# Loading a weight matrix in eight pieces instead of three, and sharing the last PSUM copy between VectorE and ScalarE

## The chip, the cores and the metric

The kernel runs on one core of a Trainium2 chip. The metric is device time in microseconds (us) of one execution. All runs named here are fast runs (granted TensorE clock 0.999 to 1.0). The kernel before was timed again beside every group of experiments; its medians lay between 1238.22 and 1238.44 us, single runs between 1238.15 and 1238.86 (the profiled execution took 1238.14). The groups did not all run on one chip, so each kernel is compared with the runs of the kernel before beside it.

## The reference, cut to what matters

Two models run on their own inputs and are joined in the last axis. `A` is a state space layer. `B` is attention over segments with a memory, followed by a projection with `Wo` (32 heads of 128, to 1024 columns). Only this projection is touched by the change:

```python
o = jnp.einsum('bhqk,bhke->bhqe', p, v)
o = jnp.einsum('bhte,hed->btd', o, Wo)      # Wo: (32, 128, 1024), 8 MB in bf16
```

## The kernel before

`Wo` is held as two halves of its columns, 128 partitions x 32 heads x 512 columns each. The first half is loaded early in the attention stage, the second when the buffers of the projections come free:

```python
for n, (hp, u) in enumerate(at):              # attention, one step at a time
    if n == 12:
        k.SP.dma_start(wo0[:], b.Wo[:, :, 0:512])
    # ... cut ...
            if first is None:
                # ... cut: wo1 allocated ...
                b.load_o_early(3)             # a DMA transpose
                for h in range(0, H, 16):
                    k.SP.dma_start(wo1[:, h:h + 16, :], b.Wo[:, h:h + 16, 512:D])
                first = b.outproj_first()     # first users of wo0 and wo1
```

The very last block of 128 rows is computed in three chunks of columns. Each is accumulated over 32 heads in one PSUM tile, copied to SBUF and stored:

```python
def out_last(self, ol):
    ot = self.p4a.tile([128, D], BF16, name="b_ost", bufs=4)
    for i, (c0, c1) in enumerate(((0, 512), (512, 768), (768, 1024))):
        p = k.ps("P")
        for h in range(H):
            k.PE.matmul(p[:, 0:c1 - c0], ol[h][:, 384:512], self.wo[...], start=(h == 0), stop=(h == H - 1))
        k.copy("vsv"[i], ot[:, c0:c1], p[:, 0:c1 - c0])   # v: VectorE, s: ScalarE
        k.SP.dma_start(self.out[0, T - 128:T, D + c0:D + c1], ot[:, c0:c1])
```

After this every engine reads a flag and branches over a fallback path that these inputs don't need.

Of the kernel before, what the change touches and what calls it, by code (L numbers as in the profile page):

```python
# [25 lines left out]
H = 32; E = 128; SEG = 32; M = 8; NSEG = 64; L = M + SEG  # L26
# [326 lines left out]
class PartB:  # L353
# [461 lines left out]
    def out_last(self, ol):  # L815

        k = self.k
        ot = self.p4a.tile([128, D], BF16, name="b_ost", bufs=4)
        for i, (c0, c1) in enumerate(((0, 512), (512, 768), (768, 1024))):
            p = k.ps("P")  # L820
            for h in range(H):
                k.PE.matmul(p[:, 0:c1 - c0], ol[h][:, 384:512], self.wo[c0 // 512][:, h, c0 % 512:c0 % 512 + c1 - c0], start=(h == 0), stop=(h == H - 1))
            k.copy("vsv"[i], ot[:, c0:c1], p[:, 0:c1 - c0])
            k.SP.dma_start(self.out[0, T - 128:T, D + c0:D + c1], ot[:, c0:c1])
            yield

# [188 lines left out]
def kernel_main(tc, A_x, A_Lre, A_Lim, A_Bre, A_Bim, A_Cre, A_Cim, A_logdt, A_Dskip, B_x, B_mem0, B_Wq, B_Wk, B_Wv, B_Wo, out,  # L1015
                force=False, dbg=None):
    with ExitStack() as ctx:
        k = K(tc, ctx)
# [3 lines left out]
        b = PartB(k, B_x, B_mem0, B_Wq, B_Wk, B_Wv, B_Wo, out)  # L1022

        def pool(name, side, bufs=2):
            return tc.tile_pool(name=name, bufs=bufs, side=side, reuse_waits="tile")
# [113 lines left out]
        wo0 = t32.tile([128, H, 512], BF16, name="t32")  # L1139
# [6 lines left out]
        first, b.ol0 = None, []  # L1146
        for n, (hp, u) in enumerate(at):
            if n == 12:
                k.SP.dma_start(wo0[:], b.Wo[:, :, 0:512])
            if hp % 2 == 0 and 2 < hp + 2 < HP:  # L1150
                if u == 4:
                    vm = b.v_mem(hp // 2 + 1)
                if u in (4, 6, 8):
                    next(vm)
            if hp == 13 and u in (3, 6, 9):
                b.load_o_early(u // 3 - 1)
            want = min(18 * HP, LEAD + (n + 1) * 18 // 11)
            while done < want:
                next(pr)
                done += 1  # L1160
            if done == 18 * HP:
                if first is None:
                    xs.close()
                    b.p4a = ctx.enter_context(pool("p4a", "left", 1))
                    wo1 = b.p4a.tile([128, H, 512], BF16, name="wo1")
                    b.wo = (wo0, wo1)
                    b.load_o_early(3)
                    for h in range(0, H, 16):
                        k.SP.dma_start(wo1[:, h:h + 16, :], b.Wo[:, h:h + 16, 512:D])
                    first = b.outproj_first()  # L1170
                next(first)
                next(first)
# [30 lines left out]
@with_exitstack  # L1203
def kernel(
    ctx: ExitStack,
    tc: tile.TileContext,
    A_x: bass.AP,
    A_Lambda_re: bass.AP,
    A_Lambda_im: bass.AP,
    A_B_re: bass.AP,  # L1210
    A_B_im: bass.AP,
    A_C_re: bass.AP,
    A_C_im: bass.AP,
    A_log_dt: bass.AP,
    A_Dskip: bass.AP,
    B_x: bass.AP,
    B_mem0: bass.AP,
    B_Wq: bass.AP,
    B_Wk: bass.AP,
    B_Wv: bass.AP,  # L1220
    B_Wo: bass.AP,
    B_seg_len: bass.AP,
    out: bass.AP,
):
    assert int(B_seg_len) == SEG
    kernel_main(tc, A_x, A_Lambda_re, A_Lambda_im, A_B_re, A_B_im, A_C_re, A_C_im, A_log_dt, A_Dskip,
                B_x, B_mem0, B_Wq, B_Wk, B_Wv, B_Wo, out)
# [35 lines left out]
```

## Time and profile before

| | before |
|---|---|
| time, median of 3 | 1238.22 us |
| span of the profile | 1236.4 us |
| TensorE busy | 1226.7 us, 99% |
| TensorE's waits, all | 1.8 us, none for `Wo` |
| last matmul ends | 1232.23 us |
| last copy (VectorE, 256 columns) | 1232.26 to 1232.68 us |
| from its end to the end of the span | 3.8 us |

With an engine at 99%, the question for any change is what it does to the little time around that engine: here the end, where nothing runs beside the copy, the store and the shutdown. The shutdown is visible when one looks at the line of the final branch. The prediction took the times of the branches from there, but made nothing of SyncE's eight waits; this view of the kernel before (engine and operation, count, durations in ns, first to last start in us) belongs to the experiments below:

```profile
L1197 SPq EVENT_SEMAPHORE  x8: 17/17/17, 1233.6 to 1234.7; - x8
...
L1197 ACTq COMPARE_BRANCH  x1: 58/58/58, 1229.4 to 1229.4; - x1
...
L1197 DVEq COMPARE_BRANCH  x1: 72/72/72, 1232.9 to 1232.9; - x1
```

The first line is SyncE waiting, one after the other, for the eight completion semaphores that go round among its DMAs (in the records of the kernel before, SyncE's 406 issues use eight semaphores, 357 of the 405 steps from one issue to the next go on to the next of the eight, and 362 issues follow a recorded wait for their own semaphore). The others are the final branches: ScalarE's long before the end, VectorE's just after its last copy.

### The profile page before, as it was taken

How to read it: one execution, taken by the hardware profiler on the slowest of the kernel's cores; microseconds unless marked ns; L12 is line 12 of the kernel's file. 1: busy time of each engine (PE TensorE's matmuls, PEld its weight loads, DVE VectorE, ACT ScalarE, POOL GpSimd, SP SyncE). 2: the span in 40 equal slices, each digit the busy share in tenths (PEclk: the TensorE clock that was granted, in tenths of full speed). 3: DMA queues.
4: the chain of work that ended last, by engine and by line, in shares of the span. 5: the costliest groups of instructions: out<-in, count | busy, mean ns of one | idle time of the engine just before them, and what ended most of it. 6: DMA issues, size and time to landing. Idle time of an engine off the chain costs nothing.

```text
span 1236.4 us, 19973 instructions
## 1 busy us (share of the span) xinstructions
PE 1226.7 (99%) x8104; PEld 655.0 (53%) x8174; DVE 680.7 (55%) x1270; ACT 266.6 (22%) x694; POOL 271.8 (22%) x437
## 2 busy tenths in 40 slices
PE   9999999999999999999999999999999999999998
PEld 4444444444455555556666656555665554445444
DVE  4799999998711124666666666666666641001000
ACT  4444444443310000211112211111221110000000
POOL 4111232112322321322222222323222320000000
PEclk9999999999999999999999999999999999999999
DMA  9943455562798834855464645546574279507000
GB/s 246 246 148 93 126 141 143 154 172 89 232 306 258 248 120 95 234 125 139 96 154 109 154 108 135 127 91 132 115 151 97 62 208 234 113 17 154 18 17 27
DMA packets 321268, 174.20 MB, mean 141 GB/s; under 512 B 145882, under 2 KB 308876, under 8 KB 321172
## 3 DMA queue, kind: packets, MB, share of 16 engines
q1 hardware_dynamic: 299076, 145.33, 48.4%
q10 hardware_dynamic: 21072, 24.38, 6.1%
q0 software_dynamic: 1024, 3.17, 0.7%
q8 instruction: 65, 1.06, 0.4%
q14 instruction: 31, 0.25, 0.1%
HBM read 84.42 MB, written 53.96 MB: 112 GB/s over the span
## 4 chain that ended last, share of the span: by engine, by line
PE 94%; DVE 4%; issue 1%; DMA 0%; ACT 0%; SPq 0%; DVEq 0%
PE psP L69 80%; PE psU L69 7%; PE psS L69 3%; PE psO L69 2%; PE psR L69 1%; DVE a_pr L284 1%; DVE a_pr L274 1%; DVE a_pr L279 1%; DMA b_xr<-in_B_x_dram 0%; DVE a_n L299 0%; DVE a_h L302 0%; DVE a_fr L232 0%; DVE a_tabh L243 0%; DVE a_tabh L240 0%; ACT a_g L285 0%
## 5 line engine op out<-in xcount | busy, mean ns | idle before, releaser
L69 PE MATMUL psP<-b_xe,b_wk 128*128 128x480 bf16 (+1 forms) x1280 | 247.5, 343 | 0.0
L69 PE MATMUL psP<-b_xe,b_wq 128*128 128x480 bf16 (+1 forms) x1280 | 247.5, 343 | 0.0
L69 PE MATMUL psP<-b_wv,b_xe 128*128 128x512 bf16 (+2 forms) x1027 | 223.0, 372 | 1.3 <-ACT b_xe L94 0.2
L689 POOL TENSOR_TENSOR b_m<-b_e,maskB 99x396 bf16<-99x396 bf16 (+1 forms) x160 | 134.7, 842 | 335.4 <-ACT b_e L688 335.4
L688 ACT ACTIVATE b_e<-psS 99x396 bf16<-99x396 f32 (+3 forms) x208 | 91.5, 442 | 530.4 <-PE psS L69 530.4
L69 PEld LDWEIGHTS <-b_wk 128*128 128x128 bf16 x1280 | 119.2, 98 | 94.2
L69 PEld LDWEIGHTS <-b_wq 128*128 128x128 bf16 x1280 | 118.5, 98 | 87.7
L69 PEld LDWEIGHTS <-b_xe 128*128 128x128 bf16 x1056 | 101.9, 98 | 119.1 <-ACT b_xe L94 0.4
L96 DVE CAST b_k<-psP 128x480 bf16<-128x480 f32 (+1 forms) x192 | 97.3, 528 | 100.0 <-PE psP L69 100.0
L96 DVE CAST b_q<-psP 128x480 bf16<-128x480 f32 (+1 forms) x192 | 97.3, 529 | 92.2 <-PE psP L69 90.9
L69 PEld LDWEIGHTS <-b_ol 128*128 128x128 bf16 x864 | 84.3, 98 | 94.4
L69 PE MATMUL psU<-a_xT,a_bt 128*128 128x512 bf16 x500 | 114.1, 379 | 0.6
L69 PE MATMUL psP<-t,a_hl 128*128 128x512 bf16 x497 | 112.3, 379 | 0.8
L96 DVE CAST b_ost<-psP 128x512 bf16<-128x512 f32 (+1 forms) x17 | 11.5, 676 | 177.6 <-PE psP L69 176.6
L69 PE MATMUL psP<-wo,b_ol 128*128 128x512 bf16 (+1 forms) x440 | 91.9, 364 | 0.4
L69 PE MATMUL psP<-t,b_ol 128*128 128x512 bf16 x408 | 91.7, 379 | 0.4
L94 ACT ACTIVATE b_vst<-psP 128x512 bf16<-128x512 f32 x126 | 72.5, 589 | 76.0 <-PE psP L69 69.9
L289 POOL TENSOR_SCALAR a_tt<-a_pr,a_tabf 128x1 f32<-128x1 f32 x48 | 34.7, 723 | 245.4 <-DVE a_pr L284 245.4
L706 DVE TENSOR_TENSOR b_ob<-psO,b_accR 99x384 bf16<-99x384 f32 x160 | 86.0, 554 | 2.9 <-DVE b_accR L705 0.4
L69 PEld LDWEIGHTS <-a_bt 128*128 128x128 bf16 x512 | 49.8, 98 | 59.5
L69 PEld LDWEIGHTS <-a_hl 128*128 128x128 bf16 x512 | 49.1, 98 | 56.7
L274 DVE TENSOR_TENSOR a_pr<-psU,a_tabf 128x2048 f32<-128x2048 f32 x32 | 73.1, 2283 | 9.2 <-PE psU L69 9.1
(203 smaller groups left out, 968.5 us busy)
## 6 DMA issues: line engine op xcount, KB each, us to landing
b_v<-b_vx SPq DMA_DIRECT2D x16, 1122.0 KB
b_wv<-in_B_Wv_dram SPq DMA_DIRECT2D x16, 1024.0 KB
b_vx<-b_vst ACTq DMA_DIRECT2D x24, 544.0 KB
b_on<-b_ob SPq DMA_DIRECT2D x15, 720.0 KB
a_hs<-a_h SPq DMA_DIRECT2D x32, 256.0 KB
b_wog<-in_B_Wo_dram SPq DMA_DIRECT2D x4, 2048.0 KB
b_wq<-in_B_Wq_dram SPq DMA_DIRECT2D x16, 512.0 KB
b_wk<-in_B_Wk_dram SPq DMA_DIRECT2D x16, 512.0 KB
```

The source lines that it names most:

```text
L69: r = f(*a, **kw)
L94: self.S.activation(out, in_, ACT.Copy)
L96: self.V.tensor_copy(out, in_)
L274: V.tensor_tensor(pr[:], u[:].unsqueeze(1).to_broadcast([128, 2, 2, TB]), view(t3, [[TB + 1, 2], [TB + 1, 2], [1, TB]]), ALU.mult)
L279: V.tensor_tensor(w, w, pr[:, :, 1, :], ALU.add)
L284: V.tensor_tensor_scan(w[:, j, :], rb, w[:, j, :], 0.0 if ini is None else ini[:, j:j + 1], ALU.mult, ALU.add)
L289: G.tensor_scalar(tt[:, j:j + 1], w[:, j, TB - 1:TB], t3[:, 1, TB:TB + 1], None, ALU.mult)
L688: k.S.activation(e[:, a:b, :, 0:n], s[0:GW, a:b, :, 0:n], ACT.Exp, scale=float(E) ** -0.5, accum_out=self.accE[0:GW, j:j + 1])
L689: k.G.tensor_tensor(mv[:, a:b, :, 0:n], e[:, a:b, :, 0:n], mask[0:GW, :, 0:n].unsqueeze(2).to_broadcast([GW, b - a, 2, n]), ALU.mult)
L706: V.tensor_tensor(self.ob[:, b0:b0 + n, :], o[0:GW, 0:n, 0:E], r.unsqueeze(2).to_broadcast([GW, n, E]), ALU.mult)
```

## The change

The intent: smaller pieces of `Wo` were to be used sooner, and two engines were to copy the last 256 columns in half the time.

```diff
-            k.copy("vsv"[i], ot[:, c0:c1], p[:, 0:c1 - c0])
+            if i < 2:
+                k.copy("vs"[i], ot[:, c0:c1], p[:, 0:c1 - c0])
+            else:
+                k.copy("s", ot[:, c0 + 128:c1], p[:, 128:c1 - c0])
+                k.copy("v", ot[:, c0:c0 + 128], p[:, 0:128])
@@
-                k.SP.dma_start(wo0[:], b.Wo[:, :, 0:512])
+                for h in range(0, H, 8):
+                    k.SP.dma_start(wo0[:, h:h + 8, :], b.Wo[:, h:h + 8, 0:512])
@@
-                    for h in range(0, H, 16):
-                        k.SP.dma_start(wo1[:, h:h + 16, :], b.Wo[:, h:h + 16, 512:D])
+                    for h in range(0, H, 8):
+                        k.SP.dma_start(wo1[:, h:h + 8, :], b.Wo[:, h:h + 8, 512:D])
```

## The prediction

> **What bounds the kernel now.** I read the page first, for the shares of the engines:
>
> ```profile
> PE 1226.7 (99%) x8104; PEld 655.0 (53%) x8174; DVE 680.7 (55%) x1270; ACT 266.6 (22%) x694; POOL 271.8 (22%) x437
> ```
>
> TensorE (PE) is busy for 1226.7 us of a span of 1236.4 us. So at most 9.7 us are idle time of this engine, whatever the loads do. Next I asked who TensorE waits for, over the whole run (columns: engine and what it was about to do, whom it waited for, us in total, times, longest us):
>
> ```profile
> PE psR L69 <- DVE hpb L110: 1.3, 1, 1.3
> PE psU L69 <- DMA b_xr<-in_B_x_dram: 0.3, 1, 0.3
> PE psP L69 <- ACT b_xe L94: 0.2, 1, 0.2
> ```
>
> These are all of its waits, 1.8 us, and none names Wo. The same question asked for 460 to 1237 us, which holds both Wo loads and all their readers, has an empty answer. The rest of the 9.7 us is the launch before the first matmul, small gaps of 0.05 us between matmuls, and the stretch after the last matmul. That end I read from the chain that ended last (start us, us, what):
>
> ```profile
> 1220.97 11.27 PE psP L69 x83
> 1232.23 0.02 issue
> 1232.26 0.42 DVE b_ost L96
> ```
>
> The last matmul ends at 1232.23, one VectorE copy of 0.42 us follows, and the remaining 3.7 us to 1236.4 are the store of 64 KB, its confirmation and the shutdown. So there are two places where this change could act: a wait for Wo, which does not exist, and a copy of 0.42 us.
>
> To see how far Wo is from being waited for, I compared the timeline of the issues on SyncE with that of TensorE. The issues (first half of the columns of Wo, then the second half in two pieces, with a DMA transpose between them):
>
> ```profile
> 510.35 0.37 SPq L69 DMA_DIRECT2D t<-in_B_Wo_dram  x1
> ...
> 999.77 0.40 SPq L69 DMA_DIRECT2D wo<-in_B_Wo_dram  x1
> 1000.27 10.73 SPq L69 DMA_TRANSPOSE b_ol<-b_on  x1
> 1011.06 0.57 SPq L69 DMA_DIRECT2D wo<-in_B_Wo_dram  x1
> ```
>
> The first readers on TensorE (`t` holds the first half, `wo` the second; heads 0 to 15 are multiplied with `b_wv`, 16 to 23 with `b_vst`, 24 to 31 with `b_ol`):
>
> ```profile
> 999.57 1.89 PE L69 MATMUL psP<-t,b_wv 128*128 128x512 bf16 x7
> ...
> 1030.05 3.62 PE L69 MATMUL psP<-wo,b_wv 128*128 128x512 bf16 x16
> 1033.50 1.89 PE L69 MATMUL psP<-wo,b_vst 128*128 128x512 bf16 x7
> ```
>
> The first half is issued 489 us before its first reader. The last piece of the second half is issued 1033.50 - 1011.06 = 22.4 us before its own.
>
> [...]
>
> **The change part by part.**
>
> *Wo, first half.* One DMA of 4096 KB becomes four of 1024 KB, same bytes, same row length of 1 KB, same queue. Three more issues at about 0.4 us are 1.2 us of SyncE, which is free from 510.72 us to its next issue at 517.62. Against 489 us of slack: 0 us.
>
> *Wo, second half.* Two DMAs of 2048 KB become four of 1024 KB. The instruction order shows one piece before the transpose and three after it. So only heads 0 to 7 go before the transpose, where 0 to 15 did; but the total of bytes up to the end of Wo is the same. In busy time by stretches of 5 us the DMA moved 246 to 347 GB/s between 1010 and 1020 us; at 284 GB/s (stretch 1005 to 1010), an estimate, 1 MiB takes 3.7 us. If the three pieces were issued at 1011 as the one is now, 3 MiB would land 11.1 us later, at about 1022; heads 8 to 15 are first read at 1030.05 + 8 x 0.216 = 1031.8, and heads 16 to 23 at 1033.5. Slack 8 us or more, so 0 us on the end.
>
> *Semaphores.* Eight completion semaphores go round among the DMAs of SyncE: each DMA waits for the one eight places earlier. More pieces shift this rotation. In the build the second half's successors, the transposes of `b_ol`, each wait for a piece of Wo. The four that fill the next tile are issued from 1020.90 to 1038.77 (17.87 us) in the kernel before, and that tile is first read at 1057.67, 19 us later. A delay of a few us stays hidden. After the first half the next weights are issued at 530.96 and first read at 565.10, 34 us later. Again 0 us.
>
> *The order on the engines.* TensorE and GpSimd keep the same instructions in the same order, VectorE too with one copy narrowed from 256 to 128 columns; ScalarE has one copy of 128 columns more.
>
> *The last copy.* Durations of the same tile's copies in this trace (columns: engine, line, op, tile, durations in ns min/median/max, then times and forms):
>
> ```profile
> L96 DVE CAST b_ost<-psP x17: 425/692/693, 1019.9 to 1232.3; 128x512 bf16<-128x512 f32 x16, 128x256 bf16<-128x256 f32 x1
> L94 ACT ACTIVATE b_ost<-psP x16: 384/597/598, 1037.2 to 1228.8; 128x512 bf16<-128x512 f32 x15, 128x256 bf16<-128x256 f32 x1
> ```
>
> VectorE: 692 ns at 512 columns, 425 at 256, so 1.043 ns a column and 158 ns fixed; at 128 columns 292 ns. ScalarE: 597 and 384, so 0.832 ns a column and 171 ns fixed; at 128 columns 277 ns. [...] Side by side, the pair would take about 0.29 us against 0.425, a gain of 0.13 us. But in the build the ScalarE copy comes first in the program, waits for TensorE, and **the VectorE copy waits for ScalarE**, and no longer for TensorE; the store waits for VectorE. They run one after the other: 0.277 + 0.03 handoff + 0.292 = 0.60 us, where the handoff is that from ScalarE to VectorE at 1136.32 to 1136.35 us in this trace. Against 0.425 us that is **+0.17 us**, all of it on the path, as nothing runs beside it.
>
> Sum: 0 + 0 + 0 + 0.17 us, from 1238.22 to **1238.4 us**.
>
> **The rivals.** *The copies overlap.* The intent of the change; then the end is 0.13 us earlier, 1238.1 us. Against it stand the wait in the build[...]. *Wo was a hidden limit and its pieces release TensorE earlier.* Then TensorE would show a wait for it; it shows none, and the total of its idle time excludes over 0.8% even if every gap went. *The rearranged queue makes a new wait:* the transposes of `b_ol` or the first pieces come late, because they wait for more semaphores. For it speaks that the DMA share is near 1 from 1015 to 1060 us. If it happened it would cost some us at about 1031 or 1057 us: 1240 to 1243 us. The slacks of 8 and 19 us speak against it. *The longer tail meets the shutdown:* ScalarE's final branch, at 1229.4 us now, moves to about 1232.9; VectorE's is at 1232.9 already and SyncE still waits for the store after it, so ScalarE should not become last. At most some tenths.
>
> **Range and chances.** The three runs before lie within 0.11 us, the known effect is +0.17 us, and an overlap would be -0.13 us. I widen to 1237.7 to 1239.4 for run to run and chip to chip differences and a small part of the third rival. Faster by over 2% is out of reach of the 9.7 us; slower by over 2% would need 25 us of new waits: 1% each at most.
>
> **What would show it.** Right: TensorE's waits unchanged and none naming Wo; the tail with ScalarE at about 0.28 us and VectorE after it at 0.29 us; the span 0.1 to 0.3 us longer; the first `wo` matmul still at about 1030 us. Wrong: two copies starting at the same time (then the wait did not hold), an entry of Wo or `b_ol` among TensorE's waits, the first `wo` matmul moved by over 1 us, or the gap after the last copy changed from 3.7 us.

The sum was 0 + 0 + 0 + 0.17 = +0.17 us, and the 0.17 comes from copies in the trace. The 0.216 us for a matmul of 512 columns is the trace's too: the 16 with `wo` and `b_wv` start at 1030.05 us and the next group at 1033.50.

## The result, and the profile after

The changed kernel took 1238.93 us (median of 4, 1238.75 to 1239.23), the kernel before beside it 1238.26 (1238.2 to 1238.33): +0.67 us, the ranges apart. The ratio is 1.0006 with a 95% interval of 0.9988 to 1.0023. Ratios are the mean time of one kernel's fast runs over that of the other's of the same rounds, so not quite the ratio of the medians. A second measurement later gave 1238.75 against 1238.34, +0.41 us, with ranges that overlap (1238.63 to 1239.18, 1238.21 to 1238.86). So the change, meant to save time, costs about half a microsecond.

TensorE after the change: its share in the page, then all of its waits.

```profile
PE 1226.5 (99%) x8104; PEld 654.5 (53%) x8174; DVE 680.6 (55%) x1270; ACT 266.8 (22%) x695; POOL 271.8 (22%) x437
```

```profile
PE psR L69 <- DVE hpb L110: 1.3, 1, 1.3
PE psU L69 <- DMA b_xr<-in_B_x_dram: 0.7, 1, 0.7
```

There is no wait for `Wo`, as there was none before; only the wait of the launch for `b_xr` is 0.4 us longer, and the 0.2 us for ScalarE are gone. The `Wo` issues in SyncE's timeline:

```profile
510.52 5.90 SPq L69 DMA_DIRECT2D t<-in_B_Wo_dram  x4
...
999.98 0.40 SPq L69 DMA_DIRECT2D wo<-in_B_Wo_dram  x1
1000.49 6.72 SPq L69 DMA_TRANSPOSE b_ol<-b_on  x1
1007.26 3.52 SPq L69 DMA_DIRECT2D wo<-in_B_Wo_dram  x3
```

Behind the shorter first piece the issue of the transpose takes 6.72 us where it took 10.73, and the rest of `Wo` is issued at 1007.26 instead of 1011.06. That buys nothing, as in TensorE's timeline its first reader stands where it stood:

```profile
1030.26 3.62 PE L69 MATMUL psP<-wo,b_wv 128*128 128x512 bf16 x16
```

1030.26 against 1030.05 is the offset of 0.21 us that this execution has from its launch on. Now the end of the chain that ended last:

```profile
1221.18 11.27 PE psP L69 x83
1232.45 0.02 issue
1232.47 0.29 ACT b_ost L94
1232.76 0.02 issue
1232.78 0.29 DVE b_ost L96
```

In the timeline, VectorE's copy names what it waited for:

```profile
1232.78 0.29 DVE L96 CAST b_ost<-psP 128x128 bf16<-128x128 f32 x1 [6.55 <-ACT b_ost L94]
```

The copies are not side by side: ScalarE first, VectorE after it, 0.60 us from 1232.47 to 1233.07 where one copy took 0.42. That is the +0.18 us of the prediction. But the span ends at 1237.3, 4.2 us after the last copy and not 3.8. The final branches and SyncE's eight waits after the change:

```profile
L1202 SPq EVENT_SEMAPHORE  x8: 17/17/17, 1234.0 to 1235.6; - x8
...
L1202 ACTq COMPARE_BRANCH  x1: 58/58/58, 1233.0 to 1233.0; - x1
L1202 DVEq COMPARE_BRANCH  x1: 72/72/72, 1233.4 to 1233.4; - x1
```

SyncE's last wait starts 1.1 us after its first in the kernel before, and 1.6 us after it here. ScalarE's branch has moved from 1229.4 to 1233.0, beside the last store.

The trace also holds each single update of a completion semaphore and each DMA packet. From these I cut the end of every run into pieces that add up. In every run the semaphore of the last store gets sixteen updates ("landings"), as many as the profile counts DMA engines; I take each for one engine's share of the store. A waiting instruction is recorded when its wait has ended: in the kernel before, the third of SyncE's waits starts 0.02 us after the sixteenth landing. The columns, in us: start of the copy or copies of the last chunk; their length; from their end to the fifteenth landing; from the fifteenth to the sixteenth; from the sixteenth to SyncE's eighth wait; from there to the end.

| kernel | copies start | copies | to 15th landing | 15th to 16th | to 8th wait | to the end | span |
|---|---|---|---|---|---|---|---|
| before | 1232.26 | 0.42 | 1.66 | 0.01 | 0.38 | 1.71 | 1236.44 |
| after | 1232.47 | 0.60 | 1.61 | **0.90** | **0.02** | 1.71 | 1237.31 |
| wo_only | 1232.24 | 0.42 | 1.61 | 0.02 | 0.02 | 1.71 | 1236.02 |
| rot_only | 1232.38 | 0.42 | 1.59 | 0.01 | 0.02 | 1.71 | 1236.14 |
| wo_nine | 1232.45 | 0.42 | 1.62 | 0.01 | 0.56 | 1.71 | 1236.77 |
| copy_only | 1232.54 | 0.60 | 1.65 | 0.60 | 0.38 | 1.71 | 1237.48 |
| v_twice | 1232.49 | 0.49 | 1.65 | 0.01 | 0.38 | 1.71 | 1236.73 |
| late_act | 1232.41 | 0.42 | 1.65 | 0.04 | 0.38 | 1.71 | 1236.61 |
| mid_act | 1232.60 | 0.42 | 1.66 | 0.54 | 0.38 | 1.71 | 1237.31 |
| two_banks | 1232.66 | 0.33 | 1.65 | 0.78 | 0.38 | 1.71 | 1237.52 |
| after_again | 1232.51 | 0.60 | 1.61 | 0.71 | 0.02 | 1.71 | 1237.16 |
| wo_last128 | 1232.48 | 0.29 | 1.47 | 1.29 | 0.02 | 1.71 | 1237.26 |
| wo_act_last | 1232.51 | 0.38 | 1.62 | 0.05 | 0.02 | 1.71 | 1236.30 |

Before and after differ by 0.21 (launch) + 0.18 (copies) - 0.05 + 0.89 (one late landing) - 0.36 (fewer waits after it) = 0.87 us, the difference of the spans. The two largest terms were not in the prediction's sum. The experiments are about these two.

### The profile page after: what moved, and what is told of

The parts are those of the page before. It is cut to its first block, busy times and chain, and to the rows that moved or that the text cites. A ratio compares the mean times of both kernels' runs of the same rounds, so it can differ in the third digit from the quotient of the medians.

```text
span 1237.3 us, 19978 instructions
## 1 busy us (share of the span) xinstructions
PE 1226.5 (99%) x8104; PEld 654.5 (53%) x8174; DVE 680.6 (55%) x1270; ACT 266.8 (22%) x695; POOL 271.8 (22%) x437
## 4 chain that ended last, share of the span: by engine, by line
PE 94%; DVE 4%; issue 1%; SPq 1%; DMA 0%; ACT 0%; DVEq 0%
PE psP L69 80%; PE psU L69 7%; PE psS L69 3%; PE psO L69 2%; PE psR L69 1%; DVE a_pr L284 1%; DVE a_pr L274 1%; SPq L69 1%; DVE a_pr L279 1%; DMA b_wv<-in_B_Wv_dram 0%; DVE a_n L299 0%; DVE a_h L302 0%; DVE a_fr L232 0%; DVE a_tabh L243 0%; DVE a_tabh L240 0%
```

## The experiments

**Each part alone.** Theory T was that all of the loss sits in the tail and `Wo` in pieces does nothing; W, that the pieces cost something.

`wo_only`: the changed kernel with the last copy as it was.

```diff
+            k.copy("vsv"[i], ot[:, c0:c1], p[:, 0:c1 - c0])     # in place of the shared copy
```

> Wo in eight pieces, the last copy left as one VectorE copy of 256 columns. Theory T (all of the change's +0.67 us comes from the tail): equal to before within 0.1 us (1238.26), no wait on Wo among TensorE's waits, 3.7 us from the end of the last copy to the end of the span. Rival W (the pieces or the shifted rotation of completion semaphores cost some of it, at the start or at the shutdown): 0.2 to 0.7 us above before.

Measured: 1237.93 us (5 runs, 1237.72 to 1238.07) against 1238.35 (9 runs, 1238.15 to 1238.47). Neither theory had it: the pieces alone are 0.42 us *faster*, ranges apart. TensorE's waits still name no `Wo`. SyncE's waits end sooner:

```profile
L1198 SPq EVENT_SEMAPHORE  x8: 17/17/17, 1233.6 to 1234.3; - x8
...
L1198 ACTq COMPARE_BRANCH  x1: 58/58/58, 1229.4 to 1229.4; - x1
```

The landing is at 1234.29 us (1234.35 in the kernel before), and the eighth wait starts 0.02 us after it, not 0.38.

`copy_only`: the kernel before with the shared copy.

```diff
+                k.copy("s", ot[:, c0 + 128:c1], p[:, 128:c1 - c0])   # in place of one VectorE copy of 256
+                k.copy("v", ot[:, c0:c0 + 128], p[:, 0:128])
```

> Wo in three pieces, the last copy shared as in the changed kernel. T: as the changed kernel, about 1238.9 us, the two copies one after the other (0.28 + 0.03 + 0.29 us). W: between the two, +0.17 us at most over before.

Measured: 1239.18 us (1239.1 to 1239.41), 0.83 above before, ranges apart; more than both theories said. The two parts, -0.42 and +0.83, add up to +0.41, which is what the second measurement of the whole change gave (the first, +0.67).

**Where do the pieces win?** SyncE's final waits take the eight semaphores in the same order in the records of the kernel before and of the changed one. In the kernel before the last store has the third of them, so five waits follow its landing, 0.38 us in all (0.07 to 0.09 us from one to the next). Five more DMAs earlier in the program (eight pieces for three) shift the round by five, and the last store gets the eighth: the other seven waits are done while it is still in flight. This is theory R; P is that smaller pieces themselves win.

`wo_nine`: as `wo_only`, with one more piece.

```diff
-                    for h in range(0, H, 8):
-                        k.SP.dma_start(wo1[:, h:h + 8, :], b.Wo[:, h:h + 8, 512:D])
+                    for h, n9 in ((0, 8), (8, 8), (16, 8), (24, 4), (28, 4)):
+                        k.SP.dma_start(wo1[:, h:h + n9, :], b.Wo[:, h:h + n9, 512:D])
```

> Wo in nine pieces in place of eight, last copy as in the kernel before. Theory R (the 0.4 us that eight pieces won come from which of the eight completion semaphores the last store gets: SyncE waits for the eight in a fixed order at the end, and each further wait after the landing costs 0.07 us; before the last store has the third, with eight pieces the eighth): nine pieces give it the first, seven waits follow the landing, so 0.15 us slower than before, 1238.5 us. Rival P (smaller pieces themselves win): 1237.9 us or less.

`rot_only`: the kernel before, with five small DMAs that nobody reads.

```diff
                 k.SP.dma_start(wo0[:], b.Wo[:, :, 0:512])
+                dm = b.p3a.tile([128, 5, 64], BF16, name="x_dm", bufs=1)
+                for j in range(5):
+                    k.SP.dma_start(dm[:, j, :], b.Wo[:, j, 0:64])
```

> Wo in three pieces as before, and five additional DMAs of 16 KB into a scratch tile beside the first of them, which shift the round of the completion semaphores by five, as eight pieces do. R: as with eight pieces, 1237.95 us, SyncE's eight waits at the end finish 0.4 us sooner. P: as before, 1238.35 us.

Measured: `wo_nine` 1238.38 us (1238.24 to 1238.54), `rot_only` 1237.90 (1237.84 to 1238.01), the kernel before 1238.44 (1238.21 to 1238.57). Five DMAs that do nothing win 0.54 us, as much as the pieces do; a ninth piece gives the gain back. P is refuted. Nothing before the end was won: the last copy starts no earlier in `rot_only` (1232.38 us) than in the kernel before (1232.26). In `wo_nine` the first wait is the one that lasts, and seven follow its end:

```profile
L1198 SPq EVENT_SEMAPHORE  x8: 17/17/17, 1234.5 to 1235.1; - x8
```

In the traces R holds: 0.02, 0.38 and 0.56 us from the landing to the eighth wait for place eight, three and one, so the place of the last store in the round is worth up to 0.54 us. With landings 0.04 to 0.07 us sooner than in the kernel before, the profiles of `wo_only`, `rot_only` and `wo_nine` give -0.41, -0.43 and +0.13 us; measured were -0.42, -0.54 and -0.06. So the time of `wo_nine` missed the forecast of 0.15 us above before: the two ranges overlap, and why it is 0.2 us under what its waits give is not explained.

**Where does the shared copy lose 0.83 us?** The longer copies account for 0.18. Nearly all of the rest is that the sixteenth landing comes 0.60 us after the fifteenth, in the changed kernel 0.90, in the kernel before 0.01. One of the sixteen shares of the store is late. The first idea (A): ScalarE, busy until the end, now reaches its final branch beside the store, and its instruction fetch or its exit is in the way. B: it belongs to the tile written by two engines, or is chance.

`late_act`: the kernel before, plus an extra matmul after the last one, which keeps ScalarE busy with a copy that the store does not wait for.

```diff
+            if i == 2:                                  # after the last store's issue in the program
+                r = k.ps("R")
+                k.PE.matmul(r[:, 0:128], ol[0][:, 384:512], self.wo[0][:, 0, 0:128], start=True, stop=True)
+                sc = self.p4a.tile([128, 128], BF16, name="x_sc", bufs=1)
+                k.copy("s", sc[:], r[:, 0:128])
```

> The kernel before plus one extra matmul of 128 columns into another bank after the last one, read by an extra ScalarE copy of 128 columns into a scratch tile; the store does not wait for it. Tells apart two sources of the 0.5 us by which the part after the last copy grew (3.7 to 4.2 us). A (ScalarE, busy until the end, reaches its final branch only now and its instruction fetch or its exit falls beside the store): the part after the VectorE copy grows to about 4.2 us and the time to about 1238.7. B (the growth belongs to the shared tile or is chance): it stays at 3.7 us and the time at 1238.3.

Measured: 1238.31 us (1238.12 to 1238.51), equal to before. A as I had put it is refuted, although ScalarE's branch stands where it stands in the changed kernel, at 1233.0.

`two_banks`: the last 256 columns in two PSUM tiles, so that the copies need not wait for each other.

```diff
+                p2 = k.ps("R")
+                for h in range(H):
+                    for b, x in ((p, c0), (p2, c0 + 128)):
+                        k.PE.matmul(b[:, 0:128], ol[h][:, 384:512], self.wo[1][:, h, ...], start=(h == 0), stop=(h == H - 1))
+                k.copy("s", ot[:, c0 + 128:c1], p2[:, 0:128])
+                k.copy("v", ot[:, c0:c0 + 128], p[:, 0:128])
```

> Wo in three pieces; the last 256 columns are multiplied into two PSUM tiles of 128 columns (64 matmuls of 128 columns in place of 32 of 256), one copied by ScalarE and one by VectorE, with no wait between the two copies. If the order on one bank is what made the copies serial, they now start within 0.05 us of each other and end 0.13 us sooner than before's copy; under A the part after them is still about 4.2 us, so the time is 1238.4 to 1238.7; under B 1238.2.

```profile
1232.66 0.29 DVE L96 CAST b_ost<-psP 128x128 bf16<-128x128 f32 x1 [6.26 <-PE psP L69]
1232.72 0.28 ACT L94 ACTIVATE b_ost<-psR 128x128 bf16<-128x128 f32 x1 [3.14 <-PE psR L69]
```

This timeline shows the overlap that the change was meant to have: starts 0.06 us apart, 0.33 us in all. So it was the one PSUM tile that put the copies in a row. Yet the kernel took 1239.32 us (1238.71 to 1240.28) against 1238.35 (1238.15 to 1238.47), ranges apart and slower than either theory said; again one landing is late, by 0.78 us. (Its 64 short matmuls follow each other at 0.056 us where the 32 of before took 0.109 us each, 0.1 us more in all.)

The packet records explain `late_act` and these together. After a final branch, packets of the kind "instruction" appear: 8 KB on queue 14 after those of ScalarE, VectorE and SyncE, 16 KB on queue 8 after TensorE's. ScalarE's starts 1.1 us after its branch (branch at 1229.39, packet at 1230.48 in the kernel before; 1233.03 and 1234.11 after), TensorE's about as late (1230.71 and 1231.86 before; 1232.13 and 1233.26 in `two_banks`). To take these for instruction fetches of the engine that branched is my reading of their kind and their times. The store's packets start from 0.83 to 1.15 us after its issue, unless something holds one share back:

| kernel | store's packets due (us) | instruction packet nearest to them, start to end | last packet starts | 15th to 16th landing |
|---|---|---|---|---|
| before | 1233.54 to 1233.86 | 1234.10 to 1234.75 | 1233.86 | 0.01 |
| late_act | 1233.69 to 1234.01 | 1234.11 to 1234.63 | 1234.01 | 0.04 |
| after | 1233.93 to 1234.25 | 1234.11 to 1234.76 | 1234.92 | 0.90 |
| copy_only | 1234.00 to 1234.32 | 1234.18 to 1234.74 | 1234.90 | 0.60 |
| two_banks | 1233.85 to 1234.17 | 1233.26 to 1234.40 (queue 8) | 1234.85 | 0.78 |

Where the instruction packet runs while the store's packets are due, a share of the store ends late; in `late_act` it comes 0.10 us after them. The trace shows the late share itself. The store has 128 packets of 512 bytes; in the changed kernel 120 of them start by 1234.25 us, and the last eight, one sixteenth, at 1234.753, 4 ns before the instruction packet ends at 1234.757. The DMA view of `after` counts the store's queue from 1234.26 to 1234.75 us and from 1234.75 to 1234.96 (packets, MB, share; the counts include confirmations of 4 bytes):

```profile
q1 hardware_dynamic: 1, 0.00, 0.1%
...
q1 hardware_dynamic: 9, 0.00, 7.0%
```

Theory F is that the fetch itself, at the wrong moment, holds one DMA engine for as long as it runs (0.3 to 0.7 us on queue 14 here, 1.0 to 1.5 us on queue 8 after TensorE's branch). It asked for a test that moves little but the moment.

`mid_act`: `late_act` with the extra matmul after head 28 instead of after head 31.

```diff
+                if i == 2 and h == 28:                  # inside the loop over heads
+                    # ... the same matmul and ScalarE copy ...
```

> As the kernel late_act (kernel before, one extra matmul and an extra ScalarE copy that the store does not wait for), with the extra matmul three heads earlier, so that ScalarE ends about 0.37 us sooner. Theory F (ScalarE's instruction fetch, which starts 1.1 us after its final branch and holds one DMA queue for 0.4 to 0.6 us, delays a sixteenth of the last store if it falls before or among its packets, 0.83 to 1.15 us after the issue): the fetch now falls there, one landing comes 0.4 to 0.9 us after the other fifteen, and the time is 1238.7 to 1239.1. If the growth belongs to the shared tile: 1238.35.

`v_twice`: two copies of 128 columns, both by VectorE.

```diff
+                k.copy("v", ot[:, c0 + 128:c1], p[:, 128:c1 - c0])
+                k.copy("v", ot[:, c0:c0 + 128], p[:, 0:128])
```

> Wo in three pieces; the last 256 columns copied by VectorE in two instructions of 128, ScalarE not involved and at its final branch 3.4 us sooner. F: no late landing, only the longer copy: 0.1 to 0.2 us above before, 1238.5 us. If a store that starts later is slower for another reason: 1239.0 us or more.

Measured: `mid_act` 1239.09 us (1239.01 to 1239.27) against 1238.44 (1238.21 to 1238.57), +0.65, ranges apart; `v_twice` 1238.43 (1238.34 to 1238.62), equal to before where 0.1 to 0.2 us more were expected. In `mid_act` the copy and the store are those of the kernel before, and the scratch copy is over before the store is issued (timeline):

```profile
1232.27 0.28 ACT L94 ACTIVATE x_sc<-psR 128x128 bf16<-128x128 f32 x1 [2.79 <-PE psR L69]
1232.60 0.42 DVE L96 CAST b_ost<-psP 128x256 bf16<-128x256 f32 x1 [6.29 <-PE psP L69]
```

```profile
L1202 SPq EVENT_SEMAPHORE  x8: 17/17/17, 1234.0 to 1235.6; - x8
...
L1202 ACTq COMPARE_BRANCH  x1: 58/58/58, 1232.8 to 1232.8; - x1
```

ScalarE's branch at 1232.8 puts its fetch at 1233.94 to 1234.38, over the store's packets (due 1233.88 to 1234.20), and one landing is 0.54 us late. In `late_act` the branch came 0.16 us after the store's issue, in `mid_act` 0.22 us before it: that is the difference between no loss and +0.65 us. In `v_twice` the copies take 0.49 us and ScalarE has branched at 1229.6; nothing is late. B is refuted by `mid_act`, where one engine writes the tile.

**Sum, and tries for something better.** `after_again` is the changed kernel; the other two start from `wo_only`.

> The changed kernel itself, beside the two below on one chip. The sum of its parts says 1238.35 - 0.45 (round of the semaphores) + 0.17 (copies in a row) + 0.6 to 0.9 (one landing of the store late behind an instruction fetch) = 1238.7 to 1239.0 us.

> Eight pieces of Wo; the last row block in chunks of 512, 384 and 128 columns, so the last copy is one of VectorE with 128 columns, 0.13 us shorter, and the last store 32 KB. If only the length of the copy counted: 1237.8 us. Theory F (any engine's instruction fetch beside the store delays it): with 32 short matmuls at the end TensorE's sequencer reaches its final branch later, as with two_banks, its fetch of 1.0 to 1.3 us starts near 1233.3 and meets the store's packets at 1233.4 to 1233.7: one landing 0.4 to 0.9 us late, 1238.2 to 1238.7 us.

> Eight pieces of Wo; the three last copies by ScalarE, VectorE, ScalarE in place of VectorE, ScalarE, VectorE, so the last copy is ScalarE's, 0.384 us against 0.425. F: ScalarE's branch near 1232.8, its fetch near 1233.9, just after the store's packets at 1233.5 to 1233.8: no late landing and 1237.85 us, the best of all. If the fetch does meet them: 1238.4 us or more.

```diff
# wo_last128, on wo_only
-        for i, (c0, c1) in enumerate(((0, 512), (512, 768), (768, 1024))):
+        for i, (c0, c1) in enumerate(((0, 512), (512, 896), (896, 1024))):
# wo_act_last, on wo_only
-            k.copy("vsv"[i], ot[:, c0:c1], p[:, 0:c1 - c0])
+            k.copy("svs"[i], ot[:, c0:c1], p[:, 0:c1 - c0])
```

Measured beside 1238.34 us (1238.21 to 1238.86): `after_again` 1238.75 (1238.63 to 1239.18), in the range of the sum. `wo_last128` 1239.02 (1238.41 to 1239.23): its copy is the shortest of all, 0.29 us, and its median is still 0.68 us above before, though the ranges overlap. TensorE branched at 1231.9 here and at 1230.7 in `wo_only`, so its fetch of 16 KB ran from 1233.02 to 1234.50, and the store, due from 1233.63, started its last packet at 1234.71. One landing was 1.29 us late, more than the 0.9 that I had allowed. `wo_act_last` 1238.00 (1237.69 to 1238.33), where 1237.85 was expected: nothing late, as ScalarE's fetch starts at 1234.16, 0.08 us after the store's last packet, but its 0.04 us shorter copy can't be seen against `wo_only`.

Over all thirteen profiles the rule holds without exception. In six (`after`, `after_again`, `copy_only`, `mid_act`, `two_banks`, `wo_last128`) an instruction packet runs while the store's packets are due; in each of them exactly eight of the store's packets wait, the first of them starts 3 to 14 ns before that instruction packet ends, and one landing is 0.54 to 1.29 us late. In the other seven no instruction packet runs at that time, and no landing is over 0.05 us late.

The best kernels are `wo_only` (1237.93) and `rot_only` (1237.90), 0.4 to 0.5 us under the kernel before; `wo_only` is 1.25 us under `copy_only`, timed beside it. Neither gain comes from the loads as such.

## Why the prediction was right or wrong

The time, 1238.93 us, lies in the range and within 2%. The direction was right for one of its reasons; the size was not (+0.17 said, +0.67 and +0.41 measured). That the time stayed in the range is in part luck: two effects that the sum left out, -0.36 and +0.6 to 0.9 us, have opposite signs.

- **TensorE bound, `Wo` not waited for:** right. Its waits, its first reader of `wo` and its order are as said.
- **First half of `Wo`, 1.2 us of SyncE for three more issues:** wrong in size, harmless. The four issues took 5.90 us, nearly all of the free 6.9 us, and the next issue moved by 0.21 us, like everything in that execution.
- **Second half, 0 us:** right. The pieces were issued sooner than I had assumed, which nobody used. The rival "the rearranged queue makes a new wait" failed: the four transposes of `b_ol` ran from 1019.96 to 1037.49 us, not later than before (1020.90 to 1038.77). The rate of pieces of 1 MiB was not looked at in any run.
- **Semaphores, "Again 0 us":** this step failed. I followed the shifted round only to the next readers. Its effect is at the last place where all eight are waited for: 0.38 us of waits after the landing became 0.02, so the term is -0.36 us, and `rot_only`, with the same 0.02 us in its trace, gives it without touching how `Wo` is loaded.
- **The last copy, +0.17 us:** right. 277 and 292 ns were said and measured, +0.18 us in all, and `two_banks` shows that the shared PSUM tile was the cause. The rival "the copies overlap" failed, as the wait in the build had said, and would not have won either.
- **"The longer tail meets the shutdown ... At most some tenths":** the right place and the wrong reason. I asked whether ScalarE would become the last to finish. It does not; the instruction packet that follows its branch meets the store that everything waits for, and one landing comes later than in the kernel before by 0.89, 0.70 and 0.59 us in `after`, `after_again` and `copy_only`. It stood among the rivals and had no term in the sum.
- **The prediction's own test, "the gap after the last copy changed from 3.7 us":** it did, to 4.2 (1237.31 - 1233.07).

With these two terms the sum is 0.18 - 0.36 + 0.6 to 0.9 = 0.4 to 0.7 us, which covers both measurements.

What stays open: the trace does not say on which of the sixteen DMA engines a packet ran, so that the fetch and the late share of the store used the same one is inferred: from eight of 128 packets waiting, and from the first of them starting within 14 ns of the fetch's end in all six profiles. Why a packet of the store would wait for an instruction packet is not shown. Instruction packets follow ScalarE's branch by 1.1 us, but that ScalarE waits for them is not shown either: its next instruction is recorded at 1229.9 us in the kernel before, and the packet starts at 1230.48. Of the late landings, the waiting packets explain 0.34 to 0.84 us; the other 0.02 to 0.45 us lie between the share's last packet and its landing, and are not explained. The offset of the launch (copies started between 1232.24 and 1232.54 in kernels with the same matmuls) was not followed.

## What to carry to other kernels

When one engine is busy 99% of the span, ask of a change what it does to the last few microseconds, and read these down to the branch, the store's landing and the final waits, in every engine and not only in the one that is copied on. Look when each engine comes to its final branch: where ScalarE's came 0.07 to 0.22 us before the issue of the last store, its fetch met the store and cost 0.5 to 0.9 us; where it came 0.15 us after the issue, or 3 us before, it cost nothing. And a small gain that appears when a load is cut up should be tested against DMAs that do nothing.
